# Attention scores by head on two halves of the array, maxima added inside the exponential, normalisation on ScalarE, and a new order of the work

## The chip, the cores and the metric

The kernel runs on one core of a Trainium2 chip. The metric is the device time in microseconds (us) of one execution; lower is better. PE is TensorE, PEld its weight loads, DVE VectorE, ACT ScalarE, POOL GpSimd, SP the engine that issues the DMAs.

## What is computed

Three parts one after the other, all in fp32: an attention over pooled keys and values, a feed-forward block with a gate that is a 3-tap convolution along the sequence, and a second block with a spatial gate.

```python
# batch 8, heads 8, seq 576, head_dim 64, pool 8 -> 72 pooled keys
k_p, v_p = mean of k, v over groups of 8 positions
scores = q @ k_p.T / sqrt(64);  scores -= max over the 72 keys
attn = exp(scores);  attn /= sum(attn) + 1e-9
x = attn @ v_p, heads side by side                      # (8, 576, 512)

h = relu(x @ w_in);  gate = sigmoid(conv3(h))           # d_ff 1024
x = (h * gate) @ w_out

h = gelu(x @ w_in2);  u, v = the two halves of h        # 512 each
v_n = (v - mean(v)) / sqrt(var(v) + 1e-6) * g_ln        # over the 512
v_s = w_sg @ v_n + b_sg                                 # along the sequence
out = x + (u * v_s) @ w_out2
```

## The kernel before

**Order.** All work is cut into tasks (Python generators); a task runs to its next `yield` as one step. The string `ORDER` (L23) names the task of each next step, as `s1.3`: score tile 1 of batch 3. `step` ties every instruction to the one before it on its engine, so this string is the order on each engine's queue and on SP's DMA queue. Nothing is reordered at run time. An engine waits where an input is not there yet, or where a buffer that it is to write is still being read.

**Tasks that matter here.** `k`, `K`: load and pool the keys of a batch; `K` (t_kfin) transposes them and writes them into KBT. `v`, `V`: the values. `q`, `p`: the queries, transposed into qT (t_qtr), 128 rows being two heads of 64. `s`: scores and softmax of one tile of 128 queries (the fifth tile of a batch has 64). `e`: the attention weights with keys on the partitions (batches 0 and 1 by TensorE, the later ones by a DMA through the scratch `eds` and a VectorE transposition; B_DMA = 2). `a`: weights times values. `i`, `t`: weights of the first block; `I`, `O`: its two products, chunk by chunk of 384 positions. `w`, `W`, `Q`: the weights of the second block's first product, with their sums (t_wsum, L647). `y`, `T`: its inputs. `n` (t_v2) and `u`: its products in seven parts instead of eight (a Strassen scheme), `n` with the normalisation. From `L`, `S`, `d`, `D`, `o` on: the spatial gate and the last product.

**PSUM.** Eight banks in three rings: "a" with 3, "i" with 2, "o" with 3. Scores take one "a" bank at a time; transpositions, `a` and half of `n`, `u`, `d` take from the same ring.

**Scores before (t_s).** KBT holds for each pair of heads a block of 128 rows and 144 columns: rows 0 to 63 and columns 0 to 71 for the even head, rows 64 to 127 and columns 72 to 143 for the odd one, zeros elsewhere (set once, L173). A matmul with the 128 rows of a pair of qT gives both heads' 72 scores. A tile has four of them (fp32: two records each in the trace), two to a bank. Per bank VectorE takes the maximum of each head (L429) and subtracts it (L431, L434) into the tile `e`. Then one exponential on ScalarE over 576 columns (L439), the sum (L441) and reciprocal (L443) on VectorE and the scaling on GpSimd (L448, L452).

**Normalisation before (t_v2).** After the gelu, VectorE's statistics (L783, L784), then on GpSimd 1e-6 is added (L787) and the power -1/2 taken (L788), and in the next step VectorE subtracts the mean and multiplies (L791), 512 columns, twice per task; 18 tasks.

Of the kernel before, what the change touches and what calls it, by code (L numbers as in the profile page):

```python
# [26 lines left out]
def pooled_attention_gated_mlps(  # L27
# [61 lines left out]
    def a_bank():  # L89
        return psum1.tile([128, 512], F32, tag="a", bufs=3, name="psa")  # L90
# [22 lines left out]
    LO_S = {m: dve for m in range(1, 8)}  # L113
    LO_G = [dve for i in range(NM + 1)]
    ident = const.tile([128, 128], F32, name="ident")
    small = const.tile([128, 6], F32, name="small")
    mask, mhalf = small[0:96, 0:4], small[:, 4:6]
    coef = const.tile([128, 32], F32, name="coef")

    in1_ctx = ExitStack()  # L120
    in1 = in1_ctx.enter_context(tc.tile_pool(name="in1", bufs=1))
    att_ctx = ExitStack()
    att1 = att_ctx.enter_context(tc.tile_pool(name="att1", bufs=1, side="right"))
    att2 = att_ctx.enter_context(tc.tile_pool(name="att2", bufs=2, side="right"))
    KBT = att1.tile([128, NP_, 2 * SP], F32, name="KBT")
    Vh = att1.tile([128, NP_, 128], F32R, name="Vh")
    Vl = att1.tile([128, NP_, 128], F32R, name="Vl")
    VR = att1.tile([96, NP_, 128], F32R, name="VR")
    eTh = att1.tile([128, NP_ + 2, S], F32R, name="eTh")
    eTl = att1.tile([128, NP_, S], F32R, name="eTl")  # L130
    hgs = {}

    def subtract(out, in0, hi, eng=nc.vector):
        eng.tensor_tensor(out=out, in0=in0, in1=hi.bitcast(F32), op=ALU.subtract)  # L134

    def to_f32(raw, t, tmp=None):

# [21 lines left out]
    def t_setup(*_):  # L159
        nc.gpsimd.memset(mhalf, -0.5)  # L160
        yield
        nc.scalar.activation(out=coef[:, 0:2], in_=mhalf, func=AF.Exp)
        yield
        make_identity(nc, ident)
        yield
        nc.vector.tensor_reduce(
            out=mask,
            in_=ident[0:96, 0:96].rearrange("p (k h j) -> p h k j", k=3, h=4),
            axis=AX.XY,
            op=ALU.add,  # L170
        )
        yield
        nc.gpsimd.memset(KBT, 0.0)  # L173
        for t in (Vh, Vl):
            nc.gpsimd.memset(t.bitcast(F32), 0.0)
# [81 lines left out]
    kv = {}  # L257

    def t_k(i, b):

        n = (2, 2, 1)[i]
        P = 128 if i < 2 else 64
        if b > 1:
            raw = att2.tile([128, 2, 512], F32, tag="raw", name="raw")
        else:
            raw = staged(f"st{b}", n, ((in1, "xh", XW * KC), (slot, "hg", 2 * NF * CH))[b] if i == 0 else None)
        rows_ = k[b].rearrange("h (j r) d -> (h j) (r d)", r=POOL)[256 * i:256 * i + P * n]
        nc.sync.dma_start(out=raw[0:P, 0:n], in_=rows_.rearrange("(a p) x -> p a x", p=P))
        yield
        if b == 1:  # L270
            kv["k1", i] = raw
            return
        if ("kp", b) not in kv:
            kv["kp", b] = att1.tile([128, 5, D], F32, tag="kp", name="kp")
        eng = dve if b == 0 and i != 1 else pool
        yield from pool_sum(eng, raw[:, 0:n], kv["kp", b][0:P, 2 * i:2 * i + n, :], P)

    def t_kfin(_, b):
        pa, pb = a_bank(), a_bank()
        kt = [pa[0:64, 128 * a:128 * a + 128] for a in range(4)] + [pb[0:64, 0:64]]  # L280
        if b == 1:
            for a in range(5):
                P = 128 if a < 4 else 64
                x = kv["k1", a // 2][0:P, a % 2, :]
                mm_sum(kt[a], [(x[:, D * r:D * r + D], ident[0:P, 0:P]) for r in range(POOL)])
                yield
        else:
            kp = kv["kp", b]
            for a in range(5):
                P = 128 if a < 4 else 64  # L290
                nc.tensor.transpose(kt[a], kp[0:P, a, :], ident[0:P, 0:P])
            yield
        odd = KBT[64:128, NP_ - 1, SP:2 * SP]
        nc.scalar.copy(out=KBT[0:64, :, 0:SP], in_=bass.AP(pa.tensor, pa.offset, [list(pa.ap[0])[:1] + [64], [2 * SP, NP_], [1, SP]]))
        nc.scalar.copy(out=odd[:, 0:8], in_=pa[0:64, 504:512])
        yield
        nc.vector.tensor_copy(
            out=KBT[64:128, 0:3, SP:2 * SP],
            in_=pa[0:64, 0:432].rearrange("p (a s) -> p a s", a=3)[:, :, SP:2 * SP])
        nc.vector.tensor_copy(out=odd[:, 8:SP], in_=pb[0:64, 0:64])  # L300
# [107 lines left out]
    def t_s(t, b):  # L408


        n = TT[t][1]
        qT = qTs.pop((b, t))
        e = sm = m8 = None
        for a in range(2):
            ps = a_bank()
            for x in range(2):
                p = 2 * a + x
                nc.tensor.matmul(out=ps[0:n, 2 * SP * x:2 * SP * x + 2 * SP], lhsT=qT[:, p, 0:n], rhs=KBT[:, p, :],  # L418
                                 start=True, stop=True)
            yield  # L420
# [678 lines left out]
```

## Time and profile before

| | |
|---|---|
| three runs | 980.34, 980.57, 981.23 us; median 980.57 |
| the profiled execution | 980.6 us, its span 978.8 us |
| mean granted TensorE clock | 0.988 |
| DMA | 143.61 MB, 54.0% of 16 engines' span |
| chain that ended last, by engine | PE 68%, DVE 14%, DMA 8%, SP's queue 4%, waits for nothing seen 3%, ACT 2%, POOL 2% |

The span runs from the first to the last instruction. A row of a group gives the time during which at least one of its instructions ran, then the mean of one; matmuls are pipelined, so a single one lasts longer than the distance to the next. What a matmul costs in a row of many is read from the distance of starts. In the name of a PE row, 128\*64 is the stationary operand (rows, columns), 64x144 the moving one.

### The profile page before, as it was taken

The page shows a single profiled execution, that of the slowest core. Times are in us where ns is not written, and L with a number is a line of the kernel's source. Part 1 is how long each engine was busy: PE and PEld are TensorE (multiplying, and loading weights), DVE is VectorE, ACT ScalarE, POOL GpSimd, SP SyncE. Part 2 cuts the span into 40 slices and gives each one's busy share as a digit, 9 for nine tenths or more (in the row PEclk, how much of TensorE's full clock was granted, in tenths as well). Part 3 has the DMA queues.
Part 4 walks back from the last instruction along what each step waited for, and adds up shares of the span by engine and source line. Part 5 has one row for each costly group of instructions (what it writes and reads, how often), then busy time and mean ns, then how long its engine had stood idle before and what let it go on. Part 6 is the DMA issues. An engine that isn't in the chain of part 4 may idle for free.

```text
span 978.8 us, 15842 instructions
## 1 busy us (share of the span) xinstructions
PE 925.9 (95%) x5396; PEld 843.8 (86%) x5396; DVE 785.7 (80%) x1399; ACT 530.4 (54%) x1108; POOL 564.1 (58%) x630
## 2 busy tenths in 40 slices
PE   5888899999999999999999899999999899999998
PEld 5677789989898998988899689998899889989996
DVE  5889997879788688787877469898786889797774
ACT  3656677676667576675656356655556333233211
POOL 3777797777968575475253265643653655554430
PEclk9899999999999999999999999999999999999999
DMA  9975183646746255132710685476437565566453
GB/s 236 266 225 98 47 182 105 156 142 155 186 112 164 85 138 137 49 95 68 198 40 1 121 166 131 137 209 149 124 125 231 187 211 180 148 213 185 163 175 129
DMA packets 182701, 143.61 MB, mean 147 GB/s; under 512 B 99776, under 2 KB 136924, under 8 KB 182620
## 3 DMA queue, kind: packets, MB, share of 16 engines
q1 hardware_dynamic: 182620, 142.61, 54.0%
q8 instruction: 42, 0.69, 0.3%
q14 instruction: 39, 0.32, 0.1%
HBM read 94.20 MB, written 48.37 MB: 146 GB/s over the span
## 4 chain that ended last, share of the span: by engine, by line
PE 68%; DVE 14%; DMA 8%; SPq 4%; issue 3%; ACT 2%; POOL 2%; DVEq 0%; ACTq 0%; POOLq 0%
PE psi L106 18%; PE psa L746 9%; PE pso L746 8%; PE pso L99 6%; PE pso L101 6%; PE pso L100 6%; PE psi L100 3%; PE psi L99 3%; PE psi L101 3%; DMA xb<-x2s 3%; PE psa L418 3%; PE psa L106 3%; DMA st<-in_v_dram 1%; DMA qb<-in_q_dram 1%; DVE sc L134 1%
## 5 line engine op out<-in xcount | busy, mean ns | idle before, releaser
L134 POOL TENSOR_TENSOR hg<-g,hg 128x384 fp32r<-128x384 f32 x96 | 100.9, 1057 | 77.9 <-ACT hg L579 77.2
L980 POOL TENSOR_TENSOR u<-u,tmp 128x288 f32<-128x288 f32 x64 | 61.1, 971 | 76.7 <-DVE tmp L976 67.6
L569 DVE SCALAR_TENSOR_TENSOR psi<-h,coef,psi 128x384 f32<-128x384 f32 x96 | 58.9, 614 | 31.3 <-ACT psi L567 30.7
L557 ACT ACTIVATE h<-psi 128x386 f32<-128x386 f32 (+1 forms) x96 | 47.4, 493 | 56.8 <-PE psi L106 56.5
L693 POOL TENSOR_TENSOR xb<-xb 128x768 f32<-128x768 f32 x24 | 45.7, 1905 | 47.5 <-DVE xc L134 21.4
L572 ACT ACTIVATE psi<-psi 128x384 f32<-128x384 f32 x96 | 46.0, 480 | 47.7 <-DVE psi L570 47.2
L134 POOL TENSOR_TENSOR eTl<-xb,eTh 128x512 fp32r<-128x512 f32 (+1 forms) x30 | 46.4, 1545 | 43.9 <-ACT eTh L502 41.4
L616 ACT CAST sc<-vf 128x512 fp32r<-128x512 f32 x48 | 28.9, 619 | 63.3 <-POOL vf L927 29.0
L570 DVE SCALAR_TENSOR_TENSOR psi<-h,coef,psi 128x384 f32<-128x384 f32 x96 | 59.8, 623 | 3.4
L576 DVE SCALAR_TENSOR_TENSOR g<-psi,h 128x384 f32<-128x384 f32 x96 | 52.2, 544 | 11.4 <-ACT psi L572 9.5
L418 PE MATMUL psa<-KBT,qT 128*128 128x144 f32 (+1 forms) x320 | 53.5, 300 | 7.0 <-DVE e L431 2.8
L418 PEld LDWEIGHTS psa<-KBT,qT 128*128 128x128 f32 (+1 forms) x320 | 45.0, 184 | 15.4 <-issue 5.7
L567 ACT ACTIVATE psi<-h,coef 128x384 f32<-128x384 f32 x96 | 56.3, 586 | 3.1
L579 ACT CAST hg<-g 128x384 fp32r<-128x384 f32 x96 | 47.7, 506 | 15.2 <-DVE g L576 13.7
L746 PE MATMUL psa<-xc,wc 128*128 128x384 f32 x252 | 51.5, 350 | 4.5 <-DVE xc L134 2.4
L746 PE MATMUL pso<-wc,xc 128*128 128x256 f32 x378 | 52.0, 285 | 3.8 <-POOL xc L134 2.1
L746 PE MATMUL psa<-wc,xc 128*128 128x256 f32 x378 | 51.7, 284 | 3.7 <-ACT tmp L769 2.3
L746 PEld LDWEIGHTS pso<-wc,xc 128*128 128x128 f32 x378 | 49.0, 190 | 5.2 <-ACT tmp L769 2.5
L746 PEld LDWEIGHTS psa<-wc,xc 128*128 128x128 f32 x378 | 49.1, 189 | 4.8 <-ACT tmp L769 3.1
L746 PE MATMUL pso<-xc,wc 128*128 128x384 f32 x252 | 48.6, 338 | 3.3 <-ACT tmp L813 2.0
L746 PEld LDWEIGHTS psa<-xc,wc 128*128 128x128 f32 x252 | 44.8, 196 | 6.5 <-DVE xc L134 2.7
L995 ACT CAST g<-u 128x256 fp32r<-128x256 f32 x64 | 22.1, 403 | 45.8 <-POOL u L980 35.2
(396 smaller groups left out, 3130.1 us busy)
## 6 DMA issues: line engine op xcount, KB each, us to landing
xb<-eds SPq DMA_DIRECT2D x24, 384.0 KB, 3.1
x2s<-ob SPq DMA_DIRECT2D x36, 256.0 KB, 2.3
xb<-x2s SPq DMA_DIRECT2D x48, 192.0 KB, 5.1
us<-ub SPq DMA_DIRECT2D x24, 384.0 KB, 2.7
vs<-vg SPq DMA_DIRECT2D x18, 512.0 KB, 4.8
u<-us SPq DMA_DIRECT2D x16, 576.0 KB, 5.9
vf<-vs SPq DMA_DIRECT2D x16, 512.0 KB, 4.2
out_dram<-ob SPq DMA_DIRECT2D x32, 256.0 KB, 2.5
```

Of the source, the lines that this page charges most:

```text
L99: nc.tensor.matmul(out=out_, lhsT=ah, rhs=bh, start=first, stop=False)
L100: nc.tensor.matmul(out=out_, lhsT=al, rhs=bh, start=False, stop=False)
L101: nc.tensor.matmul(out=out_, lhsT=ah, rhs=bl, start=False, stop=last)
L106: nc.tensor.matmul(out=out_, lhsT=a, rhs=b_, start=(i == 0), stop=(i == n - 1))
L134: eng.tensor_tensor(out=out, in0=in0, in1=hi.bitcast(F32), op=ALU.subtract)
L418: nc.tensor.matmul(out=ps[0:n, 2 * SP * x:2 * SP * x + 2 * SP], lhsT=qT[:, p, 0:n], rhs=KBT[:, p, :], start=True, stop=True)
L567: nc.scalar.activation(out=y, in_=tap(1), func=AF.Copy, scale=cw(1, f))
L569: nc.vector.scalar_tensor_tensor(out=y, in0=tap(0), scalar=cw(0, f), in1=y, op0=ALU.mult, op1=ALU.add)
L570: nc.vector.scalar_tensor_tensor(out=y, in0=tap(2), scalar=cw(2, f), in1=y, op0=ALU.mult, op1=ALU.add)
L576: nc.vector.scalar_tensor_tensor(out=go, in0=y, scalar=1.0, in1=tap(1), op0=ALU.add, op1=ALU.mult)
L746: nc.tensor.matmul(out=ps, lhsT=a, rhs=b_, start=first and i == 0, stop=last and i == n - 1, skip_group_check=True)
L980: pool.tensor_tensor(out=z, in0=z, in1=o, op=ALU.mult)
```

## The change

KBT loses its zero blocks and is scaled while it is copied, so the exponential needs no scale. A score tile is eight matmuls, one per head, of 64 rows and 72 columns; even heads use rows 0 to 63 and one bank, odd heads rows 64 to 127 and another, by turns; both banks are taken at once and in one step. In batches 0 and 1 VectorE takes the negative maximum, and ScalarE computes exp(score - max) with one instruction for each head, straight out of PSUM. In the other batches the subtraction and the one exponential stay. The four weight sums of each half (t_wsum) go from GpSimd to VectorE. The normalisation goes to ScalarE: scale is 1/std, the bias -mean/std comes from a new small VectorE instruction that stands in the step of GpSimd's power. ORDER is new as a whole: the same tasks, 3587 steps instead of 3617, since a score tile of batches 2 to 7 has one step less (8 instead of 9).

```diff
...
-    KBT = att1.tile([128, NP_, 2 * SP], F32, name="KBT")
+    KBT = att1.tile([128, NP_, SP], F32, name="KBT")
...
-        nc.gpsimd.memset(KBT, 0.0)
...
         nc.sync.dma_start(out=raw[0:P, 0:n], in_=rows_.rearrange("(a p) x -> p a x", p=P))
-        yield
         if b == 1:
             kv["k1", i] = raw
+        yield
+        if b == 1:
             return
...
+        odd = KBT[64:128, NP_ - 1, :]
+        even = bass.AP(pa.tensor, pa.offset, [list(pa.ap[0])[:1] + [64], [2 * SP, NP_], [1, SP]])
+        nc.scalar.activation(out=KBT[0:64], in_=even, func=AF.Copy, scale=EXP_SCALE)
+        nc.scalar.activation(out=odd[:, 0:8], in_=pa[0:64, 504:512], func=AF.Copy, scale=EXP_SCALE)
+        yield
+        for o, x in ((KBT[64:128, 0:3], pa[0:64, 0:432].rearrange("p (a s) -> p a s", a=3)[:, :, SP:2 * SP]),
+                     (odd[:, 8:SP], pb[0:64, 0:64])):
+            nc.vector.tensor_scalar(out=o, in0=x, scalar1=EXP_SCALE, scalar2=None, op0=ALU.mult)
...
-        for a in range(2):
-            ps = a_bank()
+        pss = [a_bank(), a_bank()]
+        for c in range(NP_):
             for x in range(2):
-                p = 2 * a + x
-                nc.tensor.matmul(out=ps[0:n, 2 * SP * x:2 * SP * x + 2 * SP], lhsT=qT[:, p, 0:n], rhs=KBT[:, p, :],
+                R = slice(64 * x, 64 * x + 64)
+                nc.tensor.matmul(out=pss[x][0:n, SP * c:SP * c + SP], lhsT=qT[R, c, 0:n], rhs=KBT[R, c, :],
                                  start=True, stop=True)
...
+        for x, ps in enumerate(pss):
+            sv = ps[0:n, 0:NP_ * SP].rearrange("p (c j) -> p c j", j=SP)
+            mx = m8[:, 4 * x:4 * x + 4]
+            nc.vector.tensor_reduce(out=mx[0:n], in_=sv, axis=AX.X, op=ALU.max, negate=b < B_DMA)
+            if b < B_DMA:
                 yield
+                for c in range(NP_):
+                    nc.scalar.activation(out=e[0:n, 2 * c + x, 0:SP], in_=sv[:, c], func=AF.Exp, bias=mx[0:n, c:c + 1])
+            else:
+                nc.vector.tensor_tensor(out=e[0:n, 4 * x:4 * x + 4, 0:SP], in0=sv, in1=bc(mx[0:n], 2, SP),
                                         op=ALU.subtract)
+            yield
+        if b >= B_DMA:
+            nc.scalar.activation(out=e[0:n, :, 0:SP], in_=e[0:n, :, 0:SP], func=AF.Exp)
+            yield
...
-            pool.tensor_tensor(out=o, in0=x, in1=y, op=op)
+            dve.tensor_tensor(out=o, in0=x, in1=y, op=op)
...
-        rs = stat.tile([128, 2], F32, tag="rstd", name="rstd")
+        rs = stat.tile([128, 4], F32, tag="rstd", name="rstd")
+        rs, nm = rs[:, 0:2], rs[:, 2:4]
         nc.gpsimd.tensor_scalar(out=rs, in0=mv[:, :, 1], scalar1=1e-6, scalar2=None, op0=ALU.add)
         nc.gpsimd.tensor_tensor(out=rs, in0=rs, in1=mhalf, op=ALU.pow)
+        nc.vector.scalar_tensor_tensor(out=nm, in0=mv[:, :, 0], scalar=-1.0, in1=rs, op0=ALU.mult, op1=ALU.mult)
         yield
         for j in range(2):
-            nc.vector.tensor_scalar(out=vg[:, j, :], in0=vg[:, j, :], scalar1=mv[:, j, 0:1], scalar2=rs[:, j:j + 1],
-                                    op0=ALU.subtract, op1=ALU.mult)
+            nc.scalar.activation(out=vg[:, j, :], in_=vg[:, j, :], func=AF.Identity, scale=rs[:, j:j + 1],
+                                 bias=nm[:, j:j + 1])
...
```

## Rows read from the trace of the kernel before

**Rows 1.** The page, part 1: busy us (share of span) xinstructions.
```profile
PE 925.9 (95%) x5396; PEld 843.8 (86%) x5396; DVE 785.7 (80%) x1399; ACT 530.4 (54%) x1108; POOL 564.1 (58%) x630
```

**Rows 2.** Sums by stretch: length, busy us (xinstructions) by engine, clock, DMA.
```profile
0.00:147.00 147.00, 122.55 (x742) 105.21 (x743) 126.33 (x237) 85.92 (x195) 102.90 (x151) 0.97 0.74 176
147.00:538.00 391.00, 389.23 (x2082) 353.15 (x2081) 316.60 (x579) 260.13 (x520) 252.73 (x299) 1.00 0.44 114
538.00:759.00 221.00, 204.91 (x1336) 196.04 (x1335) 171.06 (x279) 123.86 (x252) 106.06 (x85) 0.98 0.59 155
```

**Rows 3.** The chain of waits by line: 147 to 538, 538 to 759 us.
```profile
by line: PE psi L106 42.9%; PE pso L99 13.4%; PE pso L101 13.3%; PE pso L100 13.1%; PE psa L106 6.6%; PE psa L418 6.5%; issue 1.0%; PE psa L291 0.8%; DMA w2raw<-in_moe_w_in_dram 0.7%; SPq L633 0.4%; DVE g L576 0.3%; DVE sm L441 0.2%; ACT e 
...
by line: PE psa L746 19.7%; PE pso L746 18.7%; DMA xb<-x2s 13.4%; SPq L675 5.1%; issue 4.5%; DVE xb L681 4.2%; DVE xc L134 4.0%; DVE vg L791 3.9%; DVE st L783 3.3%; DVE sgc L134 2.3%; POOL xc L134 1.8%; DVE vg L774 1.5%; ACT xc L698 1.5%; D
```

**Rows 4.** Sums by stretch of line L418: length, PE, PEld, clock, DMA.
```profile
0.00:147.00 147.00, 21.34 (x120) 17.25 (x120) 0.97 0.74 176
147.00:538.00 391.00, 32.16 (x200) 27.70 (x200) 1.00 0.44 114
```

**Rows 5.** Timeline of PE at 404 us: start, us, engine, line, instruction.
```profile
404.06 0.34 PE L106 MATMUL psi<-xh,wi1hl 128*128 128x386 f32 x1
404.24 0.65 PE L418 MATMUL psa<-KBT,qT 128*128 128x144 f32 x4
...
404.86 0.29 PE L106 MATMUL psa<-eTl,Vh 128*128 128x288 f32 x1
404.99 0.29 PE L106 MATMUL psa<-eTh,Vl 128*128 128x288 f32 x1
```

**Rows 6.** Timeline of PE at 105 us, a visit to 64 rows.
```profile
105.24 0.33 PE L106 MATMUL psi<-xh,wi7hl 128*128 128x386 f32 x1
105.50 0.46 PE L478 MATMUL psa<-ident,en 64*128 64x64 f32 x4
...
106.13 0.30 PE L106 MATMUL psa<-eTl,Vh 128*128 128x288 f32 x1
```

**Rows 7.** Timeline of PE at 38 us, sixteen short records.
```profile
38.06 1.14 PE L106 MATMUL psa<-st,ident 64*64 64x64 f32 x16
```

**Rows 8.** Groups of PEld: shape, xcount, busy us, mean ns, idle before.
```profile
L418 PEld LDWEIGHTS psa<-KBT,qT 128*128 128x128 f32 x256 | 37.3, 194 | 10.9 <-issue 2.6 <-DVE qT L403 2.6 <-DVE KBT L297 1.5
...
L106 PEld LDWEIGHTS psa<-ident,st 128*64 128x64 f32 x64 | 7.2, 142 | 0.5 <-issue 0.5
...
L106 PEld LDWEIGHTS psa<-st,ident 64*64 64x64 f32 x16 | 1.0, 135 | 0.2 <-issue 0.2
```

**Rows 9.** Groups of VectorE by shape.
```profile
L429 DVE TENSOR_REDUCE mx<-psa 128x4 f32<-128x288 f32 x64 | 28.4, 444 | 5.9 <-PE psa L418 5.5
...
L791 DVE TENSOR_SCALAR vg<-vg,mv,rstd 128x512 f32<-128x512 f32 x36 | 26.9, 790 | 1.8 <-POOL rstd L788 1.8
...
L431 DVE TENSOR_TENSOR e<-psa,mx 128x288 f32<-128x288 f32 x16 | 7.3, 457 | 0.8
...
L443 DVE RECIPROCAL rs<-sm 128x8 f32<-128x8 f32 x32 | 6.5, 203 | 1.1
```

**Rows 10.** Groups of ScalarE by shape.
```profile
L567 ACT ACTIVATE psi<-h,coef 128x384 f32<-128x384 f32 x96 | 56.3, 586 | 3.1
...
L572 ACT ACTIVATE psi<-psi 128x384 f32<-128x384 f32 x96 | 46.0, 480 | 47.7 <-DVE psi L570 47.2
...
L439 ACT ACTIVATE e<-e 128x576 f32<-128x576 f32 x32 | 21.8, 681 | 12.0 <-DVE e L431 5.6 <-DVE e L434 3.4 <-POOL en L452 1.9
...
L778 ACT ACTIVATE vg<-vg 128x512 f32<-128x512 f32 x18 | 11.3, 630 | 9.2 <-DVE vg L774 9.2
...
L329 ACT COPY vr<-vq 32x64 f32<-32x64 f32 x36 | 8.7, 242 | 0.4
```

**Rows 11.** Groups of GpSimd by shape.
```profile
L788 POOL TENSOR_TENSOR rstd<-rstd,small 128x2 f32<-128x2 f32 x18 | 15.7, 875 | 1.5
...
L647 POOL TENSOR_TENSOR ws<-w2f 128x512 f32<-128x512 f32 x4 | 5.6, 1390 | 7.8 <-issue 4.9 <-DVE w2f L152 2.9
```

More of the change, by code (lines that the diff above doesn't have):

```diff
@@ L268, in t_k @@
         nc.sync.dma_start(out=raw[0:P, 0:n], in_=rows_.rearrange("(a p) x -> p a x", p=P))
+        if b == 1:
+            kv["k1", i] = raw
         yield
         if b == 1:
-            kv["k1", i] = raw
             return
@@ L292, in t_kfin @@
             yield
-        odd = KBT[64:128, NP_ - 1, SP:2 * SP]
-        nc.scalar.copy(out=KBT[0:64, :, 0:SP], in_=bass.AP(pa.tensor, pa.offset, [list(pa.ap[0])[:1] + [64], [2 * SP, NP_], [1, SP]]))
-        nc.scalar.copy(out=odd[:, 0:8], in_=pa[0:64, 504:512])
+        odd = KBT[64:128, NP_ - 1, :]
+        even = bass.AP(pa.tensor, pa.offset, [list(pa.ap[0])[:1] + [64], [2 * SP, NP_], [1, SP]])
+        nc.scalar.activation(out=KBT[0:64], in_=even, func=AF.Copy, scale=EXP_SCALE)
+        nc.scalar.activation(out=odd[:, 0:8], in_=pa[0:64, 504:512], func=AF.Copy, scale=EXP_SCALE)
         yield
[L297 to L300, printed above, removed]
+        for o, x in ((KBT[64:128, 0:3], pa[0:64, 0:432].rearrange("p (a s) -> p a s", a=3)[:, :, SP:2 * SP]),
+                     (odd[:, 8:SP], pb[0:64, 0:64])):
+            nc.vector.tensor_scalar(out=o, in0=x, scalar1=EXP_SCALE, scalar2=None, op0=ALU.mult)
     def t_v(i, b):
@@ L413, in t_s @@
         e = sm = m8 = None
-        for a in range(2):
-            ps = a_bank()
+        pss = [a_bank(), a_bank()]
+        for c in range(NP_):
             for x in range(2):
-                p = 2 * a + x
-                nc.tensor.matmul(out=ps[0:n, 2 * SP * x:2 * SP * x + 2 * SP], lhsT=qT[:, p, 0:n], rhs=KBT[:, p, :],
+                R = slice(64 * x, 64 * x + 64)
+                nc.tensor.matmul(out=pss[x][0:n, SP * c:SP * c + SP], lhsT=qT[R, c, 0:n], rhs=KBT[R, c, :],
                                  start=True, stop=True)
-            yield
-            if a == 0:
-                e = att2.tile([128, H, SP + 1], F32, tag="e", name="e")
-                sm = stat.tile([128, H], F32, tag="sm", name="sm")
-                m8 = stat.tile([128, H], F32, tag="mx", name="mx")
-                nc.gpsimd.memset(e[:, :, SP:SP + 1], 1e-9)
-                yield
-            sv = ps[0:n, 0:4 * SP].rearrange("p (x j) -> p x j", j=SP)
-            mx = m8[:, 4 * a:4 * a + 4]
-            nc.vector.tensor_reduce(out=mx[0:n], in_=sv, axis=AX.X, op=ALU.max)
-            if b < B_DMA:
-                nc.vector.tensor_tensor(out=e[0:n, 4 * a:4 * a + 4, 0:SP], in0=sv, in1=bc(mx[0:n], 2, SP),
-                                        op=ALU.subtract)
-            else:
-                nc.vector.tensor_tensor(
-                    out=e[0:n].rearrange("p (x c) j -> p c x j", x=2)[:, 2 * a:2 * a + 2, :, 0:SP],
-                    in0=sv.rearrange("p (c x) j -> p c x j", x=2),
-                    in1=bc(mx[0:n].rearrange("p (c x) -> p c x", x=2), 3, SP), op=ALU.subtract)
@@ new lines, in t_s @@
+        yield
+        e = att2.tile([128, H, SP + 1], F32, tag="e", name="e")
+        sm = stat.tile([128, H], F32, tag="sm", name="sm")
+        m8 = stat.tile([128, H], F32, tag="mx", name="mx")
+        nc.gpsimd.memset(e[:, :, SP:SP + 1], 1e-9)
+        yield
[9 more added lines that the diff above has]
+                nc.vector.tensor_tensor(out=e[0:n, 4 * x:4 * x + 4, 0:SP], in0=sv, in1=bc(mx[0:n], 2, SP),
+                                        op=ALU.subtract)
+            yield
@@ L438, in t_s @@
+        if b >= B_DMA:
+            nc.scalar.activation(out=e[0:n, :, 0:SP], in_=e[0:n, :, 0:SP], func=AF.Exp)
             yield
-        nc.scalar.activation(out=e[0:n, :, 0:SP], in_=e[0:n, :, 0:SP], func=AF.Exp, scale=EXP_SCALE)
-        yield
         nc.vector.tensor_reduce(out=sm[0:n], in_=e[0:n], axis=AX.X, op=ALU.add)
```

2 lines of the change are left out of this document (1 added, 1 removed).

## The prediction

> **What bounds the kernel now.** I read the page first: TensorE is busy 95% of the span, VectorE 80%, ScalarE 54%, GpSimd 58% [rows 1]. An average says little here, so next come the sums by stretch, cut where the work changes [rows 2]. From 147 to 538 us (attention and the first feed-forward block together) TensorE has work in flight for 389.2 of 391 us; the chain of waits of that stretch is PE lines for nine tenths, and the scores, L418, are 6.5% of it [rows 3]. Whatever TensorE is spared or given there moves the end by as much. The head (0 to 147 us) is another matter: TensorE lacks 24 us, VectorE is at 126 of 147 us. So is 538 to 759 us, the first product of the second block: TensorE lacks 16 us, and in the chain stand reloads of x2s (13.4%) and VectorE lines, the normalisation L791 with 3.9%, which is 8.6 us of 221 [rows 2, 3]. After 759 us the change does nothing but reorder.
>
> The profiled execution took 980.6 us, its span being 978.8, so 1.8 us lie around it; the median of the three runs is 980.57. Sums below are against 980.6.
>
> **Scores.** A tile is now four fp32 matmuls of 144 columns, each two records: 8 records. 120 records lie in the head and 200 in the bound stretch, so 15 tiles and 25 tiles [rows 4]. Price of a record: four start at 404.24, and the second 288-column matmul behind them starts at 404.86, the next 0.13 later; so the first of these streams from 404.73, and four records took 0.49 us, 0.122 each [rows 5]. A tile costs 0.98 us, and nothing is lost at its edges.
>
> After the change a tile is eight matmuls of 64 rows and 72 columns: 16 records. Half the columns should stream in 0.061 us. Two things are added. First, the array goes from 128 rows to 64 and back. One such visit stands at 105.50: the 386-column matmul before it started at 105.24 and streams for 0.18 (404.06 to 404.24 [rows 5]), so it was through by 105.42; the second 288-column matmul behind it starts at 106.13, so the first streams from 106.00: 0.58 us for four short records [rows 6]. A short record costs about 0.061 (16 of them in 1.14 us, less 0.22 for one's own length, over 15 steps [rows 7]), four 0.245. The visit itself is 0.34 us, and in the records no weight load goes ahead over either edge. Second, there are 16 weight loads instead of 8, and they are no shorter. A load of 128 rows and 128 columns lasts 194 ns, one of 64 columns 142 ns with 128 rows and 135 with 64 [rows 8]: rows do not matter, 64 columns are worth 52 to 59 ns, so an estimate for the pure loading of 128 columns is 0.11 us. Behind 0.122 us of streaming it was hidden; behind 0.061 it is not.
>
> No row shows two halves of the array at work at once, so I bound it. Per full tile:
> - one half after the other, loads setting the pace: 0.34 + 16 x 0.11 = 2.10 us, 1.12 more than now;
> - one after the other, streaming setting the pace: 0.34 + 16 x 0.061 = 1.32, 0.34 more;
> - halves in pairs (16 records in 8.5 steps, since a half's own two records follow each other), loads setting the pace: 0.34 + 8.5 x 0.11 = 1.28, 0.30 more;
> - pairs, loads hidden: 0.34 + 8.5 x 0.061 = 0.86, 0.12 less.
>
> The last tile of a batch has 64 query rows, hence 64-column loads (0.055): 0.86 or 1.32. I take the third value: the halves share no rows and write two banks, and in rows 5 the stream of one record and the load of the next already run side by side, so nothing I can see ties one half's load to the other's. In the bound stretch (20 full and 5 short tiles) that is 20 x 0.30 - 5 x 0.12 = +5.4 us; in the head 12 x 0.30 - 3 x 0.12 = +3.2, of which I count 1 us, since TensorE has idle time there. The ends: 25 x -0.12 = -3.0, and 20 x 1.12 + 5 x 0.34 = +24.1 with another +5 of 14.5 in the head.
>
> The Trainium skill (TensorE: Matmul & The Clock Gate, Part 3: Packing small matmuls — row/col tiling) says that matmuls on different row groups run concurrently, starting about 4 ns apart. No row here shows it; by it the first two bounds fall away. TensorEngine Tiling (Array Packing), Theoretical Speedup, in the same skill, has up to twice the speed for a contraction of 64 rows or fewer; by that alone the tile would be 0.49 us and the bound stretch 12 us shorter.
>
> Each tile also takes two of the three "a" banks at once. Their former tenants are read by VectorE, and the order puts other TensorE work between tiles (two of 40 follow another directly), so I cost that at nothing; if a tile waits out one maximum and subtraction (0.44 + 0.46 [rows 9]) every time, it is 0.9 x 25 = 22 us.
>
> **Exponentials of the first two batches.** VectorE drops 20 subtractions of 0.457 us, 9.1 us [rows 9]. ScalarE trades one exponential of 0.681 for eight on 72 columns with a bias from a tile. The nearest rows: a copy of 64 columns 0.242; what an operand from a tile adds, 0.586 - 0.480 = 0.106 for the same 384 columns [rows 10]. So 0.35 each, 2.8 a tile, +2.1 us on ScalarE, 21 us over ten tiles, beside 86 of 147 us now. VectorE is the fuller engine of the head, so I take -4 us. Bounds: all 9.1 us; or, if the tile's own chain counts (0.44 + 0.46 twice and 0.68 is 2.5 us now; 0.44 + 8 x 0.35 = 3.2 then), +0.7 x 10 = +7. The memset of KBT that goes, the scaling put into KBT's copies and the earlier registering of k's tiles change no count on a busy queue: nothing.
>
> **Normalisation.** 36 VectorE operations leave, 26.9 us at 0.790 [rows 9], with 8.6 us of them in the chain [rows 3]. 18 small ones come (nm; a reciprocal of 8 columns is 0.203), 3.7 us. ScalarE gets 36 on 512 columns with two operands from a tile: 0.630 + 2 x 0.106 = 0.84, 30 us beside 124 of 221 [rows 2, 10]; queued behind each pair are the copies L769 and L813 that free banks for TensorE. nm stands on VectorE right behind GpSimd's power in the same step, so VectorE can wait there for the power's 0.88 us [rows 11] and the addition ahead of it, and with it all additions that free banks; in the new order 14 of 18 tiles have over 1 us of other VectorE steps between the statistics and nm, the other four could lose 5 us together. I take -6: 8.6, less 1.2 for nm and as much for ScalarE's copies. Bounds: -12 (half the 27 us, TensorE lacking 16) and +6 (the four waits and a few late copies).
>
> **Weight sums.** Eight GpSimd operations of about 1.4 us [rows 11] become VectorE ones in the bound stretch, about 0.7 each: 6 us on an engine with 74 us free there. Hidden: 0, at most +2 if the first products of the next block wait for them.
>
> **New order.** The same steps, 30 fewer because a score step of six batches merges. Loads are moved on SP among each other (p1.1 and k1.0 come earlier). I give it 0, +-3.
>
> Sum: 980.6 + 5.4 + 1 - 4 - 6 = **977 us**; its own range 968 to 987.
>
> **Rivals.**
> - *Serial halves (slower).* The loads queue on one path; place: each of 25 tiles between 147 and 444 us; 1.12 us a tile. 980.6 + 24.1 + 5 - 4 - 6 = 1000 us. For it: loads of one core stand one behind another in every row, and no two are seen to run at once. Against: those all used the same rows. It decides once a pair of loads takes over 0.15 us. Chance 0.25.
> - *Pairs with hidden loads.* 980.6 - 3 - 0.5 - 4 - 6 = 967 us, if a half's load is done beside both streams. Chance 0.17. Against: the 0.11 us per load. (The Trainium skill, TensorEngine Tiling (Array Packing), Key Properties, has it that different tiles can load weights and multiply in parallel; no row here shows that.)
> - *Serial halves, short loads.* The change does not do what it says, and loads for 64 rows hide: 25 x 0.34 = +8.5, +1.7 in the head: 981. Chance 0.12.
> - *Pairs, but nothing won elsewhere.* ScalarE's longer queue and VectorE's wait for nm eat the 10 us: 987. Chance 0.08.
>
> The forecast itself has 0.38. About 0.2%, 2 us, is what a measurement of this kernel can tell from no change. Faster than 978.6: two thirds of the forecast (0.25), nearly all of the hidden loads (0.16), a fifth of the short loads (0.03) and a few serial cases with more won elsewhere (0.03): 0.47. Within: 0.13, from the forecast and the short loads. Slower: 0.40. The range 965 to 1002 leaves out half of what lies beyond the two outer rivals.
>
> **What would show it.** Two L418 records of different halves starting within 0.02 us of each other: pairs. 16 records from first start to the next full-array stream: 1.28 us for the forecast, 2.1 for serial loads, 0.86 for hidden ones. The stretch from the end of the head to the last O step longer by 5 us. VectorE about 33 us less busy before 759 us, ScalarE about 50 us more; TensorE's idle time from 563 to 759 us down by half. A drop of the granted clock in that stretch, TensorE waits for two "a" banks, or a clean 0.49 us tile would make the prediction wrong.

## The result, and the profile after

The changed kernel takes 989.31 us (median of four runs, 987.08 to 991.99), the kernel before 980.9 beside it (980.34 to 982.66): a ratio of 1.0084, 95% interval 1.0055 to 1.0112. It is 8 us slower; I forecast 977, faster than before. The profiled execution is the longest of the four, 991.99 us with a span of 990.2, so lengths in its trace are 2 to 3 us on the long side.

The page, part 1, of the changed kernel (as [rows 1]):

```profile
PE 936.8 (95%) x5716; PEld 852.3 (86%) x5716; DVE 754.7 (76%) x1369; ACT 563.1 (57%) x1214; POOL 543.4 (55%) x621
```

Sums by stretch of the changed kernel, with columns as in [rows 2]:

```profile
0.00:147.00 147.00, 125.53 (x835) 109.22 (x836) 109.77 (x206) 92.45 (x257) 94.90 (x142) 0.91 0.65 160
147.00:538.00 391.00, 389.07 (x2268) 348.48 (x2267) 319.59 (x589) 258.08 (x516) 244.25 (x298) 1.00 0.47 120
538.00:759.00 221.00, 204.26 (x1312) 195.40 (x1310) 154.35 (x260) 142.75 (x281) 98.95 (x80) 0.98 0.58 147
```

Over the whole run VectorE is 31 us less busy and ScalarE 33 more (my signs were 33 less and 50 more before 759 us). Two things were not in my sum. In the head the mean granted clock fell from 0.97 to 0.91. And from 538 to 759 us TensorE still lacks 16.7 us (16.1 before; by then the changed kernel is some 8 us late, so the work is not quite the same), though VectorE is 17 us less busy there; I had forecast that idle time down by half.

The full score tiles came out as forecast. Timeline of PE of the changed kernel at 298 us, a full tile between 386-column matmuls:

```profile
297.98 0.33 PE L106 MATMUL psi<-xh,wi3hl 128*128 128x386 f32 x1
298.25 1.11 PE L418 MATMUL psa<-KBT,qT 64*128 64x72 f32 x16
299.29 0.44 PE L106 MATMUL psi<-xh,wi4hl 128*128 128x386 f32 x1
299.57 0.34 PE L106 MATMUL psi<-xl,wi4hl 128*128 128x386 f32 x1
```

A 386-column matmul streams for 0.18 us (0.177 by many distances). So the stream before the tile ends at 298.16, and the first one behind it begins at 299.57 - 0.18 = 299.39: 1.24 us (by the exact starts) for a full tile, where I had forecast 1.28 and the old tile took 0.98. Another tile, seen through a window of 0.06 us and one of 0.22 us from 303.64 (columns: instructions, shortest/median/longest ns, first and last start):

```profile
L418 PE MATMUL psa<-KBT,qT x2: 327/327/327, 303.7 to 303.7; 64*128 64x72 f32 x2
...
L418 PE MATMUL psa<-KBT,qT x4: 272/300/327, 303.7 to 303.8; 64*128 64x72 f32 x4
```

Records start two at a time, by their exact starts 6 to 7 ns apart, one in each half; the pairs follow each other at 0.112 us, the estimate I had made of one weight load. The Trainium skill (TensorE: Matmul & The Clock Gate, Part 3: Packing small matmuls — row/col tiling) has matmuls on different row groups start about 4 ns apart; the trace agrees within 3 ns. The Trainium skill's "Up to 2×" for 64 rows (TensorEngine Tiling (Array Packing), Theoretical Speedup) is not met: 1.24 us against 0.98 is a tile a quarter longer. With the 64 stationary columns of a short tile the same pairs of 72 moving columns follow each other at 0.062 us, so with 128 it is the weight loads that set the pace, and the visit to 64 rows is paid each time.

The short tiles hold something that my sum had wrong. In the kernel before their stationary operand has 64 columns, and going there costs a visit too. Timeline of PE of the kernel before:

```profile
249.32 0.39 PE L100 MATMUL pso<-w4hl,hg 128*128 128x512 f32 x1
249.55 0.40 PE L101 MATMUL pso<-w4hl,hg 128*128 128x512 f32 x1
...
252.22 0.34 PE L106 MATMUL psi<-xh,wi4hl 128*128 128x388 f32 x1
252.49 0.70 PE L418 MATMUL psa<-KBT,qT 128*64 128x144 f32 x4
253.12 0.50 PE L99 MATMUL pso<-w5hl,hg 128*128 128x512 f32 x1
253.46 0.39 PE L100 MATMUL pso<-w5hl,hg 128*128 128x512 f32 x1
```

A 512-column matmul streams for 0.23 us (249.32 to 249.55). So the stream before the four records ends at 252.40, and the first one behind them begins at 253.46 - 0.23 = 253.23: 0.83 us for four records that stream for 0.49. A short tile, mostly two such groups, took 1.67 us before, and 1.32 where both banks are taken at once (a_pair, below), not the 0.98 that I had taken for it. In halves it takes 0.85 (forecast 0.86). So a short tile gains 0.47 us against a_pair and up to 0.82 against the kernel before, where my sum had 0.12, and the 25 tiles of the bound stretch should cost 20 x 0.26 - 5 x 0.47 = 2.8 us against a_pair and about 1.4 against the kernel before, not 5.4.

The groups of the changed kernel for the new instructions (as [rows 9, 10]):

```profile
L793 ACT ACTIVATE vg<-vg,rstd 128x512 f32<-128x512 f32 x36 | 27.4, 809 | 7.1 <-DVE rstd L790 7.0
...
L433 ACT ACTIVATE e<-psa,mx 128x72 f32<-128x72 f32 x64 | 14.8, 335 | 6.2 <-DVE mx L429 6.1
...
L790 DVE SCALAR_TENSOR_TENSOR rstd<-mv,rstd 128x2 f32<-128x2 f32 x18 | 8.2, 460 | 8.1 <-POOL rstd L789 8.0
```

Durations were near my estimates (0.809 us against 0.84; 0.335 against 0.35). The exponentials overlap, 64 of them in 14.8 us, 0.23 each, which is part of why ScalarE is less busy than I had summed. But the bias costs VectorE 0.46 us plus 8 us of waiting for GpSimd's power, and ScalarE waits another 7 us for the bias.

### The profile page after: what moved, and what is told of

It is laid out like the page before. It is cut to its first block, busy times and chain, and to the rows that moved or that the text cites. A ratio compares the mean times of both kernels' runs of the same rounds, so it can differ in the third digit from the quotient of the medians.

```text
span 990.2 us, 16567 instructions
## 1 busy us (share of the span) xinstructions
PE 936.8 (95%) x5716; PEld 852.3 (86%) x5716; DVE 754.7 (76%) x1369; ACT 563.1 (57%) x1214; POOL 543.4 (55%) x621
## 4 chain that ended last, share of the span: by engine, by line
PE 70%; DVE 9%; DMA 8%; POOL 4%; ACT 4%; SPq 3%; issue 2%; DVEq 0%; ACTq 0%; POOLq 0%
PE psi L106 19%; PE pso L746 10%; PE psa L746 9%; PE pso L99 6%; PE pso L101 6%; PE pso L100 5%; PE psi L99 3%; PE psa L418 3%; PE psi L100 3%; PE psi L101 3%; PE psa L106 3%; POOL xb L693 2%; DMA xb<-x2s 2%; DMA w0raw<-in_moe_w_out_dram 1%; DVE xc L134 1%
## 5 line engine op out<-in xcount | busy, mean ns | idle before, releaser
L982 POOL TENSOR_TENSOR u<-u,tmp 128x288 f32<-128x288 f32 x64 | 58.8, 935 | 68.6 <-DVE tmp L978 64.9
L616 ACT CAST sc<-vf 128x512 fp32r<-128x512 f32 x48 | 28.4, 619 | 57.7 <-POOL vf L929 30.5
L418 PEld LDWEIGHTS psa<-KBT,qT 64*128 64x128 f32 (+1 forms) x640 | 40.8, 188 | 19.0 <-issue 5.9
L418 PE MATMUL psa<-KBT,qT 64*128 64x72 f32 (+1 forms) x640 | 47.5, 282 | 7.4 <-DVE t L152 3.1
```

Of the source, the lines that this page charges most:

```text
L418: nc.tensor.matmul(out=pss[x][0:n, SP * c:SP * c + SP], lhsT=qT[R, c, 0:n], rhs=KBT[R, c, :], start=True, stop=True)
L982: pool.tensor_tensor(out=z, in0=z, in1=o, op=ALU.mult)
```

## The experiments

Each kernel ran beside the kernel before, 4 to 12 times. Ratios are to it; 0.1% is 1 us, and differences between two kernels below are differences of their ratios. Kernels a_... are the changed kernel with a part undone, b_... the kernel before with a part done.

### Parts undone in the changed kernel

**a_pair**: scores as before, the rest and the order as changed.

```diff
-        for c in range(NP_):
-            for x in range(2):
-                nc.tensor.matmul(out=pss[x][...], lhsT=qT[R, c, 0:n], rhs=KBT[R, c, :], ...)
+        for a in range(2):
+            for x in range(2):
+                nc.tensor.matmul(out=pss[a][...], lhsT=qT[:, 2 * a + x, 0:n], rhs=KBT[:, 2 * a + x, :], ...)
```

> The changed kernel with its order and all other parts, only the scores as before: four matmuls of 128 rows and 144 columns into two banks, keys padded with zeros again. Theory A (what the change lost is the score tiles: 1.24 us each from the stream before to the full-array stream behind, where it was 0.98, and the short ones 0.845): 32 x 0.26 - 8 x 0.135 = 7.2 us come back, 982. Theory B (the new order, or the lower granted clock in the head, lost it): 987 to 990, as the change whole.

980.1 us, ratio 0.9988 (0.9975 to 1.0): the halves cost 9.4 us (1.0084 - 0.9988). Theory B is out. But theory A's 7.2 takes an old short tile for 0.98 us; at the 1.32 that it takes here the tiles give 32 x 0.26 - 8 x 0.47 = 4.6, half of the loss. The run also says that everything else together gained 1.2 us, not 10.

**a_norm**: normalisation back on VectorE.

```diff
-        nc.vector.scalar_tensor_tensor(out=nm, in0=mv[:, :, 0], scalar=-1.0, in1=rs, ...)
...
-            nc.scalar.activation(out=vg[:, j, :], in_=vg[:, j, :], func=AF.Identity, scale=rs..., bias=nm...)
+            nc.vector.tensor_scalar(out=vg[:, j, :], in0=vg[:, j, :], scalar1=mv..., scalar2=rs..., ...)
```

> The changed kernel, only the normalisation back on VectorE (two operations of 512 columns per task, no bias instruction). If my step was right (-6 us from ScalarE) and something else ate it: 995. If the step gained nothing, since the bias waits on VectorE for GpSimd's power and ScalarE's copies come later: 989, within 1.5 of the change whole. If it lost: 986 or less.

999.96 us, ratio 1.0188 (1.0164 to 1.0212): in the new order the part is worth 10.2 us. That seemed to prove the step right, until b_norm below.

**a_exp**: the first two batches' maxima subtracted on VectorE, one exponential.

```diff
...
-                for c in range(NP_):
-                    nc.scalar.activation(out=e[0:n, 2 * c + x, 0:SP], in_=sv[:, c], func=AF.Exp, bias=mx[...])
+                nc.vector.tensor_tensor(out=..., in0=sv, in1=bc(mx[0:n], 2, SP), op=ALU.subtract)
+                if x == 1:
+                    nc.scalar.activation(out=e[0:n, :, 0:SP], in_=e[0:n, :, 0:SP], func=AF.Exp)
```

> The changed kernel, only the first two batches' maxima subtracted on VectorE again, with one exponential of 576 columns per tile. If my step was right (-4 us in the head): 993. If it gained nothing, since in the head the transfers and the order of the loads set the pace: 989. If eight exponentials held the two banks longer and cost the head time: 985.

992.18 us, ratio 1.0104 (1.0084 to 1.0124): 2 us, with intervals that overlap; between my step and nothing.

**a_order**: scores, exponentials, normalisation and weight sums all as before, only the order new (the edits above and below together; both banks of a tile are still taken in one step, and the keys are still scaled while copied).

> The new order alone: scores, exponentials, normalisation and weight sums all as before the change, in the changed kernel's order (both score banks are still taken in one step). Theory A (the score tiles are the loss, other parts and the order nothing): 981 to 983. Theory B (the order lost it): 987 or more. If the order alone would gain: below 979.

989.36 us, ratio 1.009 (1.0071 to 1.0109): the order alone, under the old parts, costs 8.8 us.

### Parts done alone in the kernel before

**b_norm**: the reverse of a_norm's edit, in the old order.

> The kernel before and its order, only the normalisation moved to ScalarE with the small bias instruction on VectorE. In the new order this part was worth 10.7 us (1000.0 without it, 989.3 with it). If it is the part itself: 970 to 975 (my step said 974.6). If the new order was built on it, and without that part its steps stand in bad places: 979 to 982, no change.

990.09 us, ratio 1.0084 (1.0067 to 1.0101). Neither of the two: the same part that gains 10 us in the new order costs 8 in the old one.

**b_exp**: the reverse of a_exp's edit, with the first bank's four exponentials in the step of the second pair of matmuls, and the keys scaled while copied.

> The kernel before and its order, only the first two batches' exponentials straight from PSUM with the maximum as bias (eight a tile, the keys scaled while copied). In the new order worth 2.9 us at the median. My step said 976.6; if ScalarE's eight instructions in the old places hold up what is queued behind them: 981 to 985.

993.06 us, ratio 1.0111 (1.0095 to 1.0127): 11 us slower, more than the expectation's upper end; chunk 8 of the first product (chunks of twelve matmuls, counted from 0) starts at 121.3 us where it was 111.3.

**b_wsum**: weight sums on VectorE.

```diff
-            pool.tensor_tensor(out=o, in0=x, in1=y, op=op)
+            dve.tensor_tensor(out=o, in0=x, in1=y, op=op)
```

> The kernel before, only the eight weight sums moved from GpSimd to VectorE, the part that no run has had alone. My step: no change, 980 to 982. If the sums hold up VectorE's first work for the second block: 983 or more.

981.26 us, ratio 1.001 (1.0002 to 1.0019): 1 us, at most 1.9; I had 0, at most 2.

### Why the normalisation gains nothing

**b_nonorm**

```diff
-            nc.vector.tensor_scalar(out=vg[:, j, :], in0=vg[:, j, :], scalar1=mv..., scalar2=rs..., ...)
+            pass
```

> The kernel before without the normalisation's 36 VectorE operations (subtraction of the mean and scaling are left out altogether; statistics and the power stay). It bounds what freeing VectorE can give in the stretch from 538 to 759 us. My step counted 8.6 us for it: 972, and 969 if more of the 27 us counts. Rival: VectorE is not what that stretch waits for, and reloads, GpSimd or ScalarE's copies are late next: 977 to 981.

977.08 us, ratio 0.9961 (0.9949 to 0.9973). Taking VectorE's 27 us of normalisation out altogether gives 3.8 us. My 8.6 us in the chain, and the 6 I took, were more than there is to win in the old order.

**b_norm_late** and **b_norm_pool**: b_norm with the bias moved.

```diff
...
-        nc.vector.scalar_tensor_tensor(out=nm, in0=mv[:, :, 0], scalar=-1.0, in1=rs, ...)
         yield
+        nc.vector.scalar_tensor_tensor(out=nm, in0=mv[:, :, 0], scalar=-1.0, in1=rs, ...)   # b_norm_late
...
+        nc.gpsimd.tensor_tensor(out=nm, in0=mv[:, :, 0], in1=rs, op=ALU.mult)               # b_norm_pool
+        nc.gpsimd.tensor_scalar(out=nm, in0=nm, scalar1=-1.0, ...)
```

> The kernel before with the normalisation on ScalarE (990.1 in that form, +8.2), but the small bias instruction stands one step later, in ScalarE's own step, so VectorE no longer waits for GpSimd's power in the middle of its queue. Theory D (VectorE's wait for the power, 7.8 us in the stretch 595 to 775, holds the additions that free banks): 982 to 984. Theory E (ScalarE's 30 us, and its own wait for the bias, stand ahead of the copies that free banks; TensorE waited 10.4 us for those copies where it was 3.7): 988 to 992.

992.41 us, ratio 1.0122 (1.0107 to 1.0138).

> As the normalisation on ScalarE alone in the old order, but the bias is made on GpSimd behind the power (two small operations), so VectorE has no part in it at all. Theory D: 980 to 983. Theory E: 988 to 992.

984.37 us, ratio 1.0038 (1.0024 to 1.0051). VectorE's part is 4.6 of b_norm's 8.4 us (theory D in part); the other 3.8 stay with ScalarE (theory E in part); the time lies between the two ranges. Moving the bias later is worse, which theory D excluded: then ScalarE does the waiting. The rows say who waits, from 595 to 775 us. Two TensorE groups, the products that need a bank freed by ScalarE's copy L769, and the new instruction, in the kernel before:

```profile
L746 PE MATMUL psa<-wc,xc 128*128 128x256 f32 x365 | 49.8, 284 | 3.7 <-ACT tmp L769 2.3 <-DVE vg L774 1.5
...
L746 PE MATMUL pso<-wc,xc 128*128 128x256 f32 x294 | 40.2, 285 | 1.4 <-ACT tmp L769 1.4
```

in b_norm_pool:

```profile
L746 PE MATMUL psa<-wc,xc 128*128 128x256 f32 x355 | 49.6, 287 | 7.1 <-ACT tmp L769 7.0
...
L746 PE MATMUL pso<-wc,xc 128*128 128x256 f32 x294 | 41.8, 290 | 2.6 <-ACT tmp L769 2.3 <-DVE vg L774 0.2
```

in b_norm:

```profile
L746 PE MATMUL psa<-wc,xc 128*128 128x256 f32 x366 | 51.8, 289 | 8.4 <-ACT tmp L769 6.3 <-DVE vg L774 1.9
...
L746 PE MATMUL pso<-wc,xc 128*128 128x256 f32 x294 | 40.7, 285 | 4.2 <-ACT tmp L769 4.1
...
L793 ACT ACTIVATE vg<-vg,rstd 128x512 f32<-128x512 f32 x30 | 22.8, 809 | 6.8 <-DVE rstd L790 6.6
```

and in b_norm_late:

```profile
L746 PE MATMUL psa<-wc,xc 128*128 128x256 f32 x366 | 51.6, 287 | 11.0 <-ACT tmp L769 10.9
...
L746 PE MATMUL pso<-wc,xc 128*128 128x256 f32 x294 | 41.6, 289 | 5.5 <-ACT tmp L769 5.5
...
L793 ACT ACTIVATE vg<-vg,rstd 128x512 f32<-128x512 f32 x30 | 22.8, 807 | 13.5 <-DVE rstd L791 13.1 <-ACT ub L829 0.2
```

TensorE's idle time before the two groups is 5.1, 9.7, 12.6 and 16.5 us: 4.6, 2.9 and 3.9 more at each step. The stretch from the second chunk's first product to the last is 162.9, 168.1, 170.6 and 173.2 us: 5.2, 2.5 and 2.6 more. Copies queued on ScalarE behind the normalisation keep TensorE waiting, and over the ladder the stretch grows by about that much (10.3 us for 11.4 of waiting). In the changed kernel the same stretch is 169.2 us, in a_norm 177.1, in a_order 176.0: the new order only makes room for ScalarE's instructions, it doesn't win back what they cost.

### Why the halves cost more than their tiles

**a_late_half** and **a_head_half**: halves only in batches 2 to 7, or only in batches 0 and 1; the other batches score with 128 rows. The new order throughout.

```diff
+        half = b >= B_DMA      # a_late_half;  b < B_DMA in a_head_half
+        if half:
...
+                    nc.tensor.matmul(out=pss[x]..., lhsT=qT[R, c, 0:n], rhs=KBT[R, c, SP * x:SP * x + SP], ...)
+        else:
...
+                    nc.tensor.matmul(out=pss[a]..., lhsT=qT[:, p, 0:n], rhs=KBT[:, p, :], ...)
```

> The changed kernel, but batches 0 and 1 (the head) score with 128 rows and 144 columns on zero-padded keys as before; batches 2 to 7 keep the halves. With the old scores throughout it took 980.1, with halves throughout 989.3. Theory A (every tile pays its 0.26 us): the 25 tiles after the head cost 20 x 0.26 - 5 x 0.135 = 4.5, so 984.6 and more. Theory C (the loss is in the head, where the clock stays at its lower level for 27 us with halves and 10 us without: the first product's chunk 8 starts 10.7 us later, and only 1.8 us are added after it): 982, and some 10 us at the lower clock in the head.

985.42 us, ratio 1.0038 (1.0023 to 1.0053): 4.9 us over a_pair. That looks like theory A's 4.5 and my forecast's 5.4, but it is neither. Batches 2 to 7 are 30 tiles, not 25: the 15 tiles before 147 us are batches 0, 1 and 2. By the tile costs above, 30 tiles give 24 x 0.26 - 6 x 0.47 = 3.4 us, which the interval allows. And the traces show where it went: chunk 15 of the first product starts at 141.9 us in a_pair, 145.6 here and 152.6 in the changed kernel; the last I product starts at 535.1, 540.4 and 547.6. So the 25 tiles of the bound stretch cost 1.6 us here and 1.8 in the changed kernel, and the rest arose in the head, where this run has 17 us at the lower clock (theory C said 10).

> The reverse: only batches 0 and 1 score in halves, batches 2 to 7 with 128 rows and 144 columns. Theory A: 15 tiles in the head, at most 12 x 0.26 - 3 x 0.135 = 2.7 us, so 983. Theory C: 988 to 990, with 24 us or more at the lower clock before 100 us.

986.48 us, ratio 1.0058 (1.0038 to 1.0078): 6.9 us over a_pair. Batches 0 and 1 are ten tiles, not 15, and by the tile costs above they add 8 x 0.26 - 2 x 0.47 = 1.1 us. Neither theory's time was met. The clock, by windows of 20 to 60 and 60 to 125 us (columns: length, PE busy, granted clock, DMA share, GB/s), in a_pair:

```profile
20.00:60.00 40.00, 35.35 (x254) 0.87 1.09 275
60.00:125.00 65.00, 59.76 (x352) 1.00 0.43 103
```

in a_head_half:

```profile
20.00:60.00 40.00, 36.10 (x280) 0.83 1.08 276
60.00:125.00 65.00, 57.89 (x372) 0.95 0.40 100
```

and in the changed kernel:

```profile
20.00:60.00 40.00, 35.88 (x259) 0.79 1.06 270
60.00:125.00 65.00, 58.28 (x387) 0.92 0.33 85
```

The clock has two levels, 2.4 GHz and half of it, so a mean of 0.79 over 40 us is 17 us at the lower one. The head has 10 us of it in a_pair (and before), 20 in a_head_half, 27 in the changed kernel. What that costs can be read up to the start of chunk 8 of the first product, at 108.8, 115.0 and 119.5 us in the three (columns as in [rows 2]; a_head_half's profiled execution, 983.97 us, is one of its shortest):

```profile
0.00:109.00 109.00, 89.46 (x577) 76.22 (x578) 84.61 (x156) 72.09 (x214) 73.79 (x115) 0.95 0.80 190
0.00:115.00 115.00, 94.51 (x657) 81.60 (x657) 84.01 (x156) 72.23 (x213) 73.22 (x115) 0.91 0.74 180
0.00:119.50 119.50, 99.44 (x672) 86.49 (x672) 84.44 (x157) 72.49 (x215) 72.71 (x114) 0.89 0.70 174
```

TensorE's busy time grows by 5.1 and 10.0 us over a_pair, its idle time by 1.0 and 0.5. Under a granted clock of 0.50 the score records of a_pair start every 0.24 us (from 33.24 us on) where they otherwise take 0.123. Hence 10 and 17 us more at the lower clock are worth up to 5 and 8.5 us, and the longer tiles about 1. So the head lost most of its time to TensorE working at half speed. Why the clock fell is another question, and the halves alone are not the answer: b_exp, which has no score in halves, shows 31 us in the same windows.

```profile
20.00:60.00 40.00, 34.89 (x222) 0.74 1.06 291
60.00:125.00 65.00, 55.76 (x308) 0.92 0.28 65
```

**a_head_twice**: a_pair with the score matmuls of batches 0 and 1 issued twice.

```diff
-                nc.tensor.matmul(out=pss[a]..., lhsT=qT[:, p, 0:n], rhs=KBT[:, p, :], ...)
+                for _ in range(1 + (b < B_DMA)):
+                    nc.tensor.matmul(out=pss[a]..., lhsT=qT[:, p, 0:n], rhs=KBT[:, p, :], ...)
```

> The changed kernel with the old scores (980.1 in that form), but in batches 0 and 1 every score matmul is issued twice: 15 x 0.98 = 14.7 us more full-array work for TensorE in the head. It prices TensorE's time there. Theory F (the halves cost the head 6.9 us since the clock stays longer at its lower level, 20 to 27 us of the head with halves in it and 10 to 17 without; the 2.7 us of longer tiles are mostly hidden): the added work is largely hidden too, 982 to 988, with no more than 17 us at the lower clock. Theory G (all of TensorE's time in the head counts): 993 to 996. My step counted a third: 985.

983.44 us, ratio 1.0038 (1.0023 to 1.0052), 4.9 us over a_pair. The added work is ten tiles, 80 records, so 9.8 us and not 14.7: half of it shows (by the intervals, a third to two thirds), where my step took a third. Theory G, which with 9.8 us would say 990, is out. So the longer tiles explain about half a microsecond of the 6.9. Its clock:

```profile
20.00:60.00 40.00, 37.04 (x273) 0.91 1.08 275
60.00:125.00 65.00, 60.50 (x374) 1.00 0.41 105
```

**a_head_both**: a_head_half, each of whose half-array tiles first gets the four matmuls of 128 rows too.

```diff
         if half:
+            for p in range(4):
+                nc.tensor.matmul(out=pss[p // 2]..., lhsT=qT[:, p, 0:n], rhs=KBT[:, p, :], ...)
```

> Batches 0 and 1 in halves (986.5 in that form), but each of their tiles first gets the four matmuls of 128 rows and 144 columns as well, into the same banks, which the halves then overwrite: 14.7 us more full-array work in the head. The same work on top of the old scores cost 3.3 us (983.4 against 980.1) and the clock was at its lower level for 6.8 us of the head. Theory F (what the halves cost there is the lower clock, which full-array work ahead of them would shorten): 984 to 987, no slower than the halves alone, with 14 us or less at the lower clock. Theory H (the halves cost by themselves, whatever the clock does): 989 to 992.

989.85 us, ratio 1.0108 (1.007 to 1.0146), with 9.8 us of added work here too: by the median theory H, by its runs not settled. Three of the seven (mean clock 0.987 to 0.988) took 985.2 to 985.9, the other four (0.978 to 0.982) 989.9 to 998.4. What lasts 985 or 998 us here goes with the clock, but no run shows that 64-row matmuls lower it.

**a_serial**: the changed kernel's matmuls in another sequence.

```diff
-        for c in range(NP_):
-            for x in range(2):
+        for x in range(2):
+            for c in range(NP_):
```

> The changed kernel with the same 64-row matmuls in another sequence: the four even heads, then the four odd ones, so that neighbours use the same half of the array. It is my rival's price: 16 steps of 0.11 and the visit, 2.1 us a full tile where the pairs take 1.24; 25 tiles after the head add about 20 x 0.86 + 5 x 0.45 = 19, so 1008 to 1015. If it makes no difference in what sequence the halves come: 989.

1001.49 us, ratio 1.0233 (1.0204 to 1.0263): 14.6 us more than by turns. Timeline of PE at 303 us:

```profile
302.98 0.33 PE L106 MATMUL psi<-xh,wi3hl 128*128 128x386 f32 x1
303.25 1.62 PE L418 MATMUL psa<-KBT,qT 64*128 64x72 f32 x16
304.79 0.44 PE L106 MATMUL psi<-xh,wi4hl 128*128 128x386 f32 x1
305.07 0.34 PE L106 MATMUL psi<-xl,wi4hl 128*128 128x386 f32 x1
```

From 303.16 to 304.89 it is 1.73 us (1.74 by the exact starts), not my rival's 2.10: the sixteen records take twelve steps of 0.112, since the odd half's first records run beside the even half's last ones. By turns instead of one half after the other is worth 0.5 us a full tile, and it comes from the sequence of issue alone.

### A version that beats both

In a_pair the last I product ended 4.5 us earlier than before, and the second block's products lost 7 us again. **h2229** takes the new order for its first 2229 steps (just into the second block's first products) and then what is left in the old order; scores and normalisation are the old ones, exponentials and weight sums the new ones. **h2379** joins 150 steps later and leaves the first chunk's normalisation on ScalarE.

```diff
-    for key in NEW:
+    done = Counter(NEW[:2229])
+    rest = [key for n, key in enumerate(OLD) if OLD[:n + 1].count(key) > done[key] and key[0] != "s"]
+    for key in NEW[:2229] + rest:
```

> Candidate from the landmarks: with old scores in the new order the first block's last I product ended 4.5 us earlier than before, and 6.7 us were lost again from the second block's second chunk to its last product. So: the new order and exponentials up to the first step of the second block's products, from there the remaining steps in the old order, with scores of 128 rows and the normalisation on VectorE. If gains by stretch add up: 975 to 977. If the old steps don't fit behind the new beginning: 980 or more.

977.47 us, ratio 0.9969 (0.9958 to 0.9981): 3 us faster than the kernel before, 11 faster than the changed one (1.0084 - 0.9969). TensorE's idle time there is again that of before:

```profile
L749 PE MATMUL psa<-wc,xc 128*128 128x256 f32 x348 | 47.6, 284 | 3.8 <-ACT tmp L772 2.3 <-DVE vg L777 1.5
...
L749 PE MATMUL pso<-wc,xc 128*128 128x256 f32 x294 | 40.3, 285 | 1.4 <-ACT tmp L772 1.4
```

> As the candidate that took 977.5 (new order first, old order from the second block's products on, old scores), but the orders are joined a chunk later, and the first chunk's six tiles normalise on ScalarE, the others on VectorE. In the new order that chunk was 1.6 us shorter than before (56.4 against 58.0 from the last I product to the second chunk). If stretches add up: 975.5 to 977. If not: 978 or more.

979.83 us, ratio 0.9994 (0.9979 to 1.0008): no gain. In its trace the first chunk is as long as in h2229 (57.7 us against 57.6 from the last I product to the second chunk), but the block's other chunks take 3.6 us longer (166.9 against 163.3).

## Why the prediction was wrong

The sum was +5.4 and +1 for the scores, -4, -6, and 0 +- 3 for the order. Against it, by the ratios and, where the text says traces, by one profiled execution of each kernel:

| step | forecast | measured |
|---|---|---|
| scores, bound stretch, 25 tiles | +5.4 | +1.8 (traces, changed - a_pair, chunk 15 to the last I product) |
| scores, head, 15 tiles | +1 | +10.7 up to there (the same traces) |
| both | +6.4 | +9.4 (changed - a_pair; 11.2 in the two traces) |
| exponentials and order, up to the last I product | -4 | -4.5 (traces, a_pair - before) |
| normalisation and order, from there to the second block's last product | -6 | +3.7 (traces, 225.0 us against 221.3 before) |
| exponentials, normalisation, sums, order together | -10 | -1.2 (a_pair) |

- **The normalisation is the step that failed.** I took -6 from VectorE's 8.6 us in the chain [rows 3]. b_nonorm shows that they are worth 3.8 if they vanish. And ScalarE's 30 us were not beside free time: I named "the copies L769 and L813 that free banks for TensorE" as queued behind them, and VectorE's wait for the power, and priced the two at 2.4 us. In the old order they cost 8.4 + 3.8 = 12 us. In the new order the stretch that was to be 6 us shorter is 3.7 longer. This is the mechanism of the rival "pairs, but nothing won elsewhere", 987 us, to which I gave 0.08; that its time is near is luck in part, since it has the scores at +6.4.
- **Scores in the head: the term was too small.** "Of which I count 1 us, since TensorE has idle time there" holds for TensorE's time: the idle time hides about half of it (a_head_twice), and the ten tiles of batches 0 and 1 are only 1.1 us longer. What I left out is the clock, although [rows 2] show it at 0.97 in the head and the prediction named only a drop after 538 us. Those ten tiles in halves cost 6.9 us; in the trace chunk 8 starts 6.2 us later, of which TensorE's busy time is 5.1, and most of that fits its 10 us more at the lower clock. Why the clock falls stays open. It is also no fixed price: over all 127 runs of the 18 kernels, comparing each run with its own kernel's mean, a microsecond more at the lower clock (twice the missing clock times the run) goes with 0.28 us more time (correlation 0.67), over the 85 runs of the kernel before beside them with 0.07 (0.34).
- **Scores, bound stretch: right in mechanism, wrong in size.** Halves in pairs, loads setting the pace, the visit to 64 rows: 1.24 us against 1.28. The rivals with serial halves and with hidden loads are out. But "nothing is lost at its edges" is wrong for the old short tiles, whose 64-column loads cost a visit as well. By the measured tile costs the term is 2.8 us against a_pair; the traces show 1.8, a third of the forecast, and the last microsecond stays open. That a_late_half measures 4.9 is no support for it: it has 30 tiles, and most of its loss arose in the head.
- **The order: not a term of its own.** I gave it 0. Alone it costs 8.8 us, the normalisation alone costs 8.4, the exponentials alone 11, and all together with the weight sums gain 1.2. My reading, not shown one by one: each part moves work to an engine whose queue was written for other work, and only an order written for the parts makes up for that. Terms that are taken from rows of the old order could not be added to an order that is new.
- **Exponentials.** -4 forecast; about 2 in the new order (overlapping intervals), +11 in the old one. **Weight sums:** about 1 us, inside the bound of 2. **"a" banks:** nothing in the bound stretch, as forecast, where TensorE's waits of all kinds are 1.7 us in the changed kernel.

## What to carry to other kernels

A share of the chain says how long an operation stood on the path, not what its removal gives: remove it in an experiment first, and price the wait that moves to the next engine. Where engines run fixed queues, moving an instruction to another engine and rewriting the order are one change, and undoing one part at a time only tells what it is worth in that order. Before two halves of the array replace a zero-padded whole, compare the weight load with the stream: here loads of 128 columns (0.112 us a pair) set the pace where 72 columns could stream in 0.061, and the sequence of issue decides how much of the two halves overlaps. When a tile is priced, look at its short forms too.

## What the runs showed of the hardware

- Weight loads of two halves proceed in parallel with each other: they start 6 to 7 ns apart like their matmuls (changed kernel, 303.76 us), and pairs of loads and of 72-column matmuls follow every 0.112 us, and every 0.062 us for 64 query rows, which makes the short tile 0.85 us.
- A visit from 128 stationary columns to 64 and back costs 0.34 us, as a visit to 64 rows does: 0.83 us for four records that stream for 0.49 (kernel before, 252 us).
- The two halves overlap even where the sequence is even heads first, then odd: four pairs of the sixteen records (a_serial).
- Extra full-array work in a head with idle time costs about half of its length, and the head then had 7 us at the lower clock instead of 10 (a_head_twice).
